# LSH attention with a gated projection on one core: a second weight pair converted in the late stage, and a whole batch taken first there

## The chip, the core and the metric

One core of one Trainium2 chip. It has TensorE (PE) for matrix products, VectorE (DVE), ScalarE (ACT), GpSimd (POOL), and SyncE (SP), whose queue issues most transfers. The metric is the device time of one execution in microseconds.

## The reference

Four batches of 8 heads, 768 tokens and 64 dimensions. q and k are hashed by the signs of six projections; a key counts for a query only where the hashes agree. The softmax over these keys weighs v, and the result, as 3072 rows of 512, goes through a gated projection whose weights come as 64-bit floats.

```
mask = q_bucket[:, :, :, None] == k_bucket[:, :, None, :]
scores = np.where(mask, scale * np.matmul(q, k.transpose(0, 1, 3, 2)), -1000000000.0)
attn = softmax(scores)                       # with 1e-09 in the divisor
x = (attn @ v).transpose(0, 2, 1, 3).reshape(B * S, H * D)
gate = 1.0 / (1.0 + np.exp(-(x @ w_gate)))   # 512 x 1536
return (gate * (x @ w_val)) @ w_out          # 1536 x 512
```

## The kernel before, in words

**Attention (to about 405 us).** 16 pairs of heads, each in two groups of three query tiles. A group has six score tasks on PE (`sc`, eight matmuls, L1551 and L1557), a minimum on DVE for each (L1569), an exponential on ACT (L1578), six tasks of transposes (`tp`, L1614), six copies out of PSUM on ACT or DVE (L1620) and six products with v (`pv`, L1630, four records each in the trace). The result is scaled (L1637) and stored as `xd`.

**Weights.** A tile of 64-bit weights (`raw`) is made into 32-bit floats by `floats` (L674): exponent and mantissa masks (L689, L697) and two combining steps (L702, L707) on DVE, one step on ACT (L692), one product (L712). The float is split into a high and a low part: a cast (L766, L830) and a subtraction (L769, L833). The weights of gate and value come in pairs of blocks (`load_pair`, a pair has two tiles each for gate and value); four sums (L821 to L824) make seven operands of a scheme with seven block products for eight, and the operands are stored in DRAM (`kept_z`, L836). The output weights have one tile for each of 12 blocks (`load_w`); those for later use are stored as `kept`. In attention, masks and combining steps run on DVE and the rest mostly on POOL; in the late stage DVE and ACT do all of it.

There are six pairs of blocks. Of the first pair the plain weights are held as well (`we`), for batch 0. Before, the first five pairs are converted in attention, the last one (`late`, L1221) in the late stage.

**The tail of attention.** Batch 0's products with the first two blocks (`moe_early`: `zg`, `zv`, `zo`) run on PE after the last `pv`. POOL and DVE split x (L867, L870) and the gated blocks (L920) for it.

**The late stage.** For each batch (`products`, L994), the pairs of blocks are visited, first the gate (g), then the value (v). A visit (`visit`, L1166) is seven products of six matmuls (L1178), whose banks ACT copies (L1186) and DVE sums (L1193); then sigmoid (L1250), gating (L1264, L1266) and a split into `gh` and `gl` (L1271, L1274). Between the products of the next two visits stand six output pieces of six matmuls (`y`, L932). The pairs' operands are fetched from DRAM into three slots by POOL's queue (`wsg`, `wsv`, L1728). Batches 1 to 3 are whole (six pairs), batch 0 has five. Before, the order is batch 0, 1, 2, 3, and a whole batch visits the first pair last.

**What sets the order.** Each piece of work is a task with a key, the tasks it follows and the buffers it takes. `Plan.order` (L400) plays the tasks through with fixed times and gives each engine its instructions in one list; PE follows a written list of task numbers, `ORDER` (L51), and `SHIFT` (L113) moves the other keys. On the chip each engine works through its list in order.

Of the kernel before, what the change touches and what calls it, by code (L numbers as in the profile page):

```python
# [507 lines left out]
def lsh_attention_glu_kernel(ctx, tc, q, k, v, proj, w_gate, w_val, w_out, out):  # L508
# [12 lines left out]
    J1 = 2
    NL = 3
    J2 = 10
    JP1, JP2, JPN = J1 // 2, J2 // 2, NJ // 2
    SL = 7
    A11, A21, A12, A22, S1, S2, S4 = range(SL)
    S3 = A21
    SCALE = 1.0 / float(D) ** 0.5
# [1248 lines left out]
```

## Time and profile before

| | us |
|---|---|
| median of 3 runs (964.59 to 965.78) | 965.33 |
| the profiled execution's own time | 965.6 |
| its span, from first to last instruction | 963.8 |
| PE / PE weight loads / DVE / ACT / POOL busy | 952.0 / 774.8 / 608.2 / 548.2 / 274.3 |
| last matmul of attention ends, early products begin | 405.3 |
| first product of the late stage | 428.7 |

The span is the time between the first and the last instruction; 1.8 us of the execution lie around it. Busy shares are means over stages with different limits, so the windows are read by stage. Matmuls are pipelined, and a busy PE can still lose time between kinds of work. The clock of PE was at its full level throughout.

### The profile page before, as it was taken

What the parts mean: (1) busy time and instruction counts of PE and PEld (TensorE: products, weight loads), DVE (VectorE), ACT (ScalarE), POOL (GpSimd) and SP (SyncE); (2) the same over time, 40 slices, a digit from 0 to 9 for tenths busy, and PEclk for the clock granted to TensorE, in tenths of its full rate; (3) what the DMA queues carried; (4) which work ended last, traced back from release to release, by engine and by line L of the source; (5) the groups of instructions that cost most, each with busy time, mean ns of one, the idle gap of its engine ahead of it and who ended that gap; (6) DMA issues with size and microseconds to landing.
All of it is one profiled execution on the core that took longest, in us unless ns stands there. A gap on an engine that the chain in (4) does not pass through costs nothing.

```text
span 963.8 us, 20105 instructions
## 1 busy us (share of the span) xinstructions
PE 952.0 (99%) x8067; PEld 774.8 (80%) x8070; DVE 608.2 (63%) x1173; ACT 548.2 (57%) x993; POOL 274.3 (28%) x325
## 2 busy tenths in 40 slices
PE   9999999999999999999999999999999999999998
PEld 5666665666666567689999999999999999999997
DVE  7999898999899898676656743334633336333332
ACT  5988898898888889554334433324433235333322
POOL 4444655666765665630000000000000000000000
PEclk9999999999999999999999999999999999999999
DMA  7666888888897877489966774444744444644421
GB/s 186 175 194 189 224 252 241 244 249 238 263 268 213 233 228 228 171 315 411 370 237 230 280 262 175 153 153 154 271 170 158 170 177 173 222 154 153 154 78 66
DMA packets 116606, 204.37 MB, mean 212 GB/s; under 512 B 63456, under 2 KB 87968, under 8 KB 110624
## 3 DMA queue, kind: packets, MB, share of 16 engines
q1 hardware_dynamic: 107456, 118.08, 39.9%
q0 software_dynamic: 6688, 84.42, 23.7%
q8 instruction: 63, 1.03, 0.4%
q10 hardware_dynamic: 2368, 0.59, 0.3%
q14 instruction: 31, 0.25, 0.1%
HBM read 147.84 MB, written 43.42 MB: 198 GB/s over the span
## 4 chain that ended last, share of the span: by engine, by line
PE 92%; DVE 4%; DMA 2%; ACT 1%; issue 1%; SPq 0%; ACTq 0%; DVEq 0%
PE y L932 20%; PE pv L1630 12%; PE zBg L1178 10%; PE zBv L1178 10%; PE sc L1557 9%; PE tp L1614 7%; PE zDv L1178 5%; PE zDg L1178 5%; PE sc L1551 4%; PE zAg L1178 2%; PE zAv L1178 2%; PE h L1452 1%; DVE e L1569 1%; PE zg L896 1%; PE zv L896 1%; PE idle L642 1%
## 5 line engine op out<-in xcount | busy, mean ns | idle before, releaser
L1569 DVE TENSOR_SCALAR_CACHE_REDUCE e<-sc 128x768 f32<-128x768 f32 x192 | 177.1, 952 | 20.3 <-PE sc L1557 18.5
L1578 ACT ACTIVATE e<-e,st 128x768 f32<-128x768 f32 x192 | 178.9, 933 | 15.1 <-DVE e L1569 13.2
L932 PE MATMUL y<-wo,gh 128*128 128x512 f32 x480 | 151.0, 396 | 0.0
L1630 PE MATMUL pv<-e,vr 128*64 128x384 f32 x768 | 140.7, 496 | 0.0
L1620 ACT COPY e<-tp 128x768 f32<-128x768 f32 x144 | 112.2, 795 | 27.9 <-PE tp L1614 27.1
L1614 PEld LDWEIGHTS tp<-ident,e 64*128 64x128 f32 x2304 | 87.0, 138 | 45.7 <-issue 13.7
L1178 PE MATMUL zBg<-x,wsg 128*128 128x384 f32 x552 | 111.0, 335 | 0.0
L1178 PE MATMUL zBv<-x,wsv 128*128 128x384 f32 x552 | 110.7, 335 | 0.0
L1178 PEld LDWEIGHTS zBg<-x,wsg 128*128 128x128 f32 x552 | 98.2, 188 | 6.6 <-ACT t1g L1186 0.4
L1178 PEld LDWEIGHTS zBv<-x,wsv 128*128 128x128 f32 x552 | 98.3, 188 | 6.0
L932 PEld LDWEIGHTS y<-wo,gh 128*128 128x128 f32 x480 | 89.9, 187 | 15.2
L1614 PE MATMUL tp<-ident,e 64*128 64x64 f32 x2304 | 99.6, 226 | 1.8 <-DVE e L1569 0.9
L1271 ACT CAST gh<-zt 128x384 fp32r<-128x384 f32 x92 | 47.1, 514 | 95.1 <-DVE zt L1266 75.5
L932 PE MATMUL y<-wo,gl 128*128 128x512 f32 x240 | 93.2, 388 | 0.0
L1557 PE MATMUL sc<-kh,ql 64*128 64x384 f32 x192 | 89.8, 468 | 0.0
L1557 PE MATMUL sc<-kh,qsl 64*128 64x384 f32 x192 | 89.8, 468 | 0.0
L1630 PEld LDWEIGHTS pv<-e,vr 128*64 128x64 f32 x768 | 48.2, 136 | 51.3 <-issue 43.0
L1728 POOL DMA_DIRECT2D wsv<-kzv x23 | 12.2, 532 | 236.9 <-PE zDg L1178 224.6
L1728 POOL DMA_DIRECT2D wsg<-kzg x23 | 12.3, 536 | 227.4 <-PE zDv L1178 206.9
L1250 ACT ACTIVATE sig<-sig 128x384 f32<-128x384 f32 x69 | 36.2, 525 | 61.7 <-DVE sig L1193 61.6
L1274 DVE TENSOR_TENSOR gl<-zt,gh 128x384 fp32r<-128x384 f32 x92 | 51.0, 554 | 29.2 <-ACT gh L1271 29.2
L1551 PE MATMUL sc<-kq 64*128 64x384 bf16 x384 | 64.8, 328 | 2.3 <-ACT e L1620 1.1
(214 smaller groups left out, 1964.4 us busy)
## 6 DMA issues: line engine op xcount, KB each, us to landing
wsg<-kzg POOLq DMA_DIRECT2D x23, 1792.0 KB, 8.1
wsv<-kzv POOLq DMA_DIRECT2D x23, 1792.0 KB, 7.6
kzg<-wkg SPq DMA_DIRECT2D x12, 896.0 KB
kzv<-wkv SPq DMA_DIRECT2D x12, 896.0 KB
rawg<-in_moe_w_gate_dram SPq DMA_DIRECT2D x14, 512.0 KB
rawv<-in_moe_w_val_dram SPq DMA_DIRECT2D x14, 512.0 KB
vr<-in_v_dram SPq DMA_DIRECT2D x16, 384.0 KB
rb<-rd SPq DMA_DIRECT2D x64, 96.0 KB
```

The source lines that it names most:

```text
L932: nc.tensor.matmul(acc, a[:, slot, ts_], w, start=(first and i == 0), stop=(last and i == 2), skip_group_check=cols != slice(None),)
L1178: nc.tensor.matmul(acc, streams[n, jp][:, c, wa, a_], X[x_][:, xa, c], start=first and c == 0 and i == 0, stop=c == 1 and i == 2, skip_gro ...
L1250: lambda blk=blk: nc.scalar.activation(sig[:, blk], w["B"][:, :GN] if blk == 2 else sig[:, blk], AF.Sigmoid),
L1271: nc.scalar.copy(side["h"][:, blk], w["z", blk])
L1274: eng.tensor_sub(side["l"][:, blk], w["z", blk], f(side["h"][:, blk]))
L1551: nc.tensor.matmul(sc[:, j, :GN], kq[z["h"]][rows, 2 + 2 * g + h, t * P : (t + 1) * P], kq[z["h"]][rows, h], start=True, stop=False, tile_ ...
L1557: nc.tensor.matmul(sc[:, j, :GN], q_[rows, c], z["k" + x][rows, h * GN : (h + 1) * GN], start=False, stop=(m == 2), tile_position=(j * D, 0),)
L1569: nc.vector.tensor_scalar(sp(e), gz["sc", t, h][:, :, :GN], -MASKED * SCALE, None, op0=ALU.min, op1=ALU.min, accum_out=gz["st", t][:, h : ...
L1578: nc.scalar.activation(e, e, AF.Exp, bias=st[:, h : h + 1], scale=-1.0, accum_out=gz["su"][:, h * GT + t : h * GT + t + 1],)
L1614: nc.tensor.transpose(tp[:, r, at_ : at_ + D], gz["e", t, h][rows, c * P : (c + 1) * P], ident[rows, rows], tile_position=(r * D, 0),)
L1620: copy(gz["e"][:, :, c * P : (c + 1) * P].rearrange("p n (r d) -> p r n d", r=2), gz["tp", c][:, :, :GN].rearrange("p r (n d) -> p r n d", ...
L1630: nc.tensor.matmul(gz["pv"][rows, :GN], z["v"][:, h, c], gz["e"][:, h * GT : (h + 1) * GT, c * P : (c + 1) * P], start=(c == 0), stop=(c = ...
```

## The change

Four things, and with them new lists `ORDER` and `SHIFT`:

1. `J2` goes from 10 to 8: four of the six pairs are converted in attention, two in the late stage (12 tiles there instead of 6). Their tasks get the key -2 instead of 1000, just ahead of the -1 of the late stage's other DVE work.
2. The late stage takes batch 1, a whole one, first, then 0, 2, 3, and a whole batch visits the pairs in order. The output weights of the first two blocks stay where they are; those of the last two are converted late, stored, and fetched once into the slots of `raw`.
3. The sums of the first pair start from the early weights, high plus low part (`joined`, on POOL), in place of loading and converting the tiles again.
4. The low part is written over the float itself and stored from there, and the float has two buffers; every store is cut into one for the high and one for the low part.

```
-SLOTS = ("two", "one", "e", "st", "su", "sv", "rb", "xs", "vr", "h", "raw2")
+SLOTS = ("two", "one", "e", "st", "su", "sv", "rb", "xs", "vr", "h", "raw2", "mid1", "mid2")
...
-    3, 4, 5, 6, 7, 8, 9, 10, 11, 12, 13, 14, 15, 39, 16, 17, 18, 42, 19, 20, 48, 21, 45, 51, 22, 23, 24, 25, 26, 53,
...
+    3, 4, 5, 6, 7, 8, 9, 10, 11, 12, 13, 14, 15, 16, 39, 17, 18, 19, 42, 20, 21, 22, 48, 45, 51, 23, 24, 25, 26, 27,
...
-    J2 = 10
+    J2 = 8
...
-        raw1=1, mid1=1, raw2=2, mid2=1, wk=1, xr=1, x2=1, x3=1, ob=3,
+        raw1=1, mid1=2, ex1=1, raw2=2, mid2=2, ex2=1, wk=1, xr=1, x2=1, x3=1, ob=3,
...
-            z["all"] = stage().tile([P, SL * P], I32, name=f"mf{name}", tag="wmf", bufs=stock["mid" + own])
+            z["all"] = stage().tile([P, SL * P], I32, name=f"mf{name}", tag=f"wmf{slot['mid' + own]}", bufs=1)
...
-        early = j if j < J1 else j - NJ + J1 if j >= NJ - J1 else None
+        early = j if j < J1 else None
...
+        away = last and n == "o" and j >= NJ - J1
...
+                z["h"] = (later["w"] if last else stage1).tile([P, SL * P], F32R, name=f"w{n}{j}", tag="wk", bufs=1)[:, :N_EL]
+            if "w" in z:
+                z["h"], z["l"] = z["w"][:, 0], z["w"][:, 1]
+            else:
+                z["l"] = z["mf"].bitcast(F32R)
...
+        elif away:
+            s_ = [
+                dma(key, 262144, lambda: keep(0), after=[h]),
+                dma(key, 262144, lambda: keep(1), after=[made[n, j]], give=["mid" + own]),
+            ]
+            add(FIRST, "sp", 0, lambda: None, after=[s_[0], made[n, j]], give=["wk2"])
+            made[n, j] = dma(1e3, 524288, fetch, after=[*s_, *everything], take=["raw2"])
+        else:
...
+            y["l"] = y["f"].bitcast(F32R)
+            eng.tensor_sub(y["l"], y["f"], f(y["h"]))
...
+        def joined():
+            z["all"] = stage1.tile([P, SL * P], I32, name=f"mf{n}{jp}_{c}", tag=f"wmf{slot['mid1']}", bufs=1)
+            of = streams["e"][:, "gv".index(n)].rearrange("p j a (h c m) -> a c p h j m", h=2, m=P)
+            to = f(z["all"])[:, :N_EL].rearrange("p (h j m) -> p h j m", h=2, j=2)
+            for h in range(2):
+                nc.gpsimd.tensor_add(to[:, h], f(of[0, c])[:, h], f(of[1, c])[:, h])
+
+        if jp < JP1:
+            z, own = {}, "1"
+            e = add(key, "pool", 1340, joined, after=[made[n, 0], made[n, 1]], take=["mid1"], port=0.92)
+        else:
+            z, e, own = floats(key, load, [last or score_tasks[at_n]], last, f"{n}{jp}_{c}")
...
+        s_ = [dma(key, 458752, lambda: keep(0), after=[h]), dma(key, 458752, lambda: keep(1), after=[m], give=["mid" + own])]
+        add(FIRST, "sp", 0, lambda: None, after=[s_[0], m], give=["wk2" if last else "wk"])
...
-        jps = list(range(JP1, JPN)) + list(range(JP1)) * whole_
+        jps = list(range(JP1 * (not whole_), JPN))
...
+                    for w_ in line:
+                        if len(w_) == 2:
+                            load_w(-2, *w_, False, m1)
+                        else:
+                            everything.append(load_pair(-2, *w_, m1))
...
-    for b in range(B):
-        prev = products(2e4 + b, b, prev, ends)
+    for m, b in enumerate([B - NL, *range(B - NL), *range(B - NL + 1, B)]):
+        prev = products(2e4 + m, b, prev, ends)
```

The lists move instructions on every engine. At the end of attention, on PE, before (`tp` are transposes, `pv` products with v; the numbers are batch, group and chunk):

```order
L1614 MATMUL tp_3_0_2_7382<-ident,e_3_0_7048 128x64 x12
L1614 MATMUL tp_3_0_3_7396<-ident,e_3_0_7048 128x64 x12
L1630 MATMUL pv_3_0_7373<-e_3_0_7048,vr_3_7001 64x384 x2
L1614 MATMUL tp_3_1_0_7420<-ident,e_3_1_7245 128x64 x12
L1614 MATMUL tp_3_0_4_7436<-ident,e_3_0_7048 128x64 x12
L1630 MATMUL pv_3_0_7373<-e_3_0_7048,vr_3_7001 64x384 x2
L1614 MATMUL tp_3_1_1_7455<-ident,e_3_1_7245 128x64 x12
L1614 MATMUL tp_3_1_2_7468<-ident,e_3_1_7245 128x64 x12
L1614 MATMUL tp_3_1_3_7482<-ident,e_3_1_7245 128x64 x12
L1630 MATMUL pv_3_0_7373<-e_3_0_7048,vr_3_7001 64x384 x2
L1630 MATMUL pv_3_1_7502<-e_3_1_7245,vr_3_7001 64x384 x6
L1614 MATMUL tp_3_0_5_7517<-ident,e_3_0_7048 128x64 x12
```

and after, at the same place:

```order
L1665 MATMUL tp_3_0_1_7271<-ident,e_3_0_7029 128x64 x12
L1665 MATMUL tp_3_0_2_7285<-ident,e_3_0_7029 128x64 x12
L1681 MATMUL pv_2_1_7061<-e_2_1_6809,vr_2_6579 64x384 x2
L1681 MATMUL pv_3_0_7303<-e_3_0_7029,vr_3_6990 64x384 x4
L1681 MATMUL pv_2_1_7061<-e_2_1_6809,vr_2_6579 64x384 x2
L1681 MATMUL pv_3_0_7303<-e_3_0_7029,vr_3_6990 64x384 x2
L1665 MATMUL tp_3_0_3_7315<-ident,e_3_0_7029 128x64 x12
L1665 MATMUL tp_3_1_0_7331<-ident,e_3_1_7178 128x64 x12
L1665 MATMUL tp_3_0_4_7346<-ident,e_3_0_7029 128x64 x12
L1681 MATMUL pv_2_1_7061<-e_2_1_6809,vr_2_6579 64x384 x2
L1681 MATMUL pv_3_0_7303<-e_3_0_7029,vr_3_6990 64x384 x2
L1665 MATMUL tp_3_1_1_7367<-ident,e_3_1_7178 128x64 x12
```

The products with v stand in fewer and longer runs; over the whole of attention PE changes its kind of work 383 times before and 368 times after, up to the first product of the late stage.

On DVE in the late stage, the gate visit whose sums have the most conversion work around them, before (`sig` are the sums that free a bank of PE, the others convert weights):

```order
L1193 TENSOR_TENSOR sig<-zAg_0_8390,t1g_0_8403 128x384
L689 TENSOR_SCALAR exv_0_8420<-rawv_0_8160 128x512
L697 TENSOR_SCALAR mfv_0_8423<-rawv_0_8160 128x512
L702 SCALAR_TENSOR_TENSOR mfv_0_8423<-rawv_0_8160,mfv_0_8423 128x512
L707 SCALAR_TENSOR_TENSOR exv_0_8420<-rawv_0_8160,exv_0_8420 128x512
L712 TENSOR_TENSOR mfv_0_8423<-mfv_0_8423,exv_0_8420 128x512
L821 TENSOR_TENSOR mfv_0_8423<-mfv_0_8423 128x128
L822 TENSOR_TENSOR mfv_0_8423<-mfv_0_8423 128x128
L823 TENSOR_TENSOR mfv_0_8423<-mfv_0_8423 128x128
L824 TENSOR_TENSOR mfv_0_8423<-mfv_0_8423 128x128
L1193 TENSOR_TENSOR sig<-zDg_0_8426,t167g_0_8452 128x384
L1193 TENSOR_TENSOR sig<-zDg_0_8426,t16g_0_8434 128x384
```

and after, in the fifth pair of the first batch:

```order
L1241 TENSOR_TENSOR sig<-zAg_1_8537,t1g_1_8544 128x384
L732 SCALAR_TENSOR_TENSOR exg_0_8494<-rawg_0_8405,exg_0_8494 128x512
L737 TENSOR_TENSOR mfg_0_8548<-mfg_0_8548,exg_0_8494 128x512
L863 TENSOR_TENSOR mfg_0_8548<-mfg_0_8548 128x128
L864 TENSOR_TENSOR mfg_0_8548<-mfg_0_8548 128x128
L865 TENSOR_TENSOR mfg_0_8548<-mfg_0_8548 128x128
L866 TENSOR_TENSOR mfg_0_8548<-mfg_0_8548 128x128
L714 TENSOR_SCALAR exo_8590<-rawo_8484 128x512
L722 TENSOR_SCALAR mfo_8592<-rawo_8484 128x512
L876 TENSOR_TENSOR mfg_0_8548<-mfg_0_8548,wkg_8588 128x896
L727 SCALAR_TENSOR_TENSOR mfo_8592<-rawo_8484,mfo_8592 128x512
L1241 TENSOR_TENSOR sig<-zDg_1_8569,t167g_1_8603 128x384
```

Between a visit's first and second sum (`zAg`, `zDg`) stand ten instructions in place of nine, now with a low part and steps of the next tile in one row, and in the whole of the second to fifth pair 93 conversion instructions beside the 56 own ones, and two for x.

On POOL at the end of attention, before (`mf`, `wk`: conversion of the first pair; `gl`, `xh`, `xl`: the early products; `wsg`: the first fetch of the late stage):

```order
L821 TENSOR_TENSOR mfg_0_7506<-mfg_0_7506 128x128
L822 TENSOR_TENSOR mfg_0_7506<-mfg_0_7506 128x128
L823 TENSOR_TENSOR mfg_0_7506<-mfg_0_7506 128x128
L824 TENSOR_TENSOR mfg_0_7506<-mfg_0_7506 128x128
L830 CAST wkg_7574<-mfg_0_7506 128x896
L833 TENSOR_TENSOR wkg_7574<-mfg_0_7506,wkg_7574 128x896
L920 TENSOR_TENSOR gl<-gf_0_0_7643,gh 128x384
L867 CAST xh_1_7659<-xr_1_2591 128x384
L870 TENSOR_TENSOR xl_1_7660<-xr_1_2591,xh_1_7659 128x384
L867 CAST xh_1_7659<-xr_1_2591 128x384 x3
L870 TENSOR_TENSOR xl_1_7660<-xr_1_2591,xh_1_7659 128x384
L1728 DMA wsg_46_7712<-kzg_130 128x3584
```

and after:

```order
L1636 TENSOR_SCALAR su_148<-su_148 128x6
L1636 TENSOR_SCALAR su_149<-su_149 128x6
L976 TENSOR_TENSOR gl<-gf_0_0_7540,gh 128x384
L923 CAST xh_1_7553<-xr_1_2520 128x384
L926 TENSOR_TENSOR xl_1_7554<-xr_1_2520,xh_1_7553 128x384
L923 CAST xh_1_7553<-xr_1_2520 128x384
L926 TENSOR_TENSOR xl_1_7554<-xr_1_2520,xh_1_7553 128x384
L1779 DMA wsg_46_7580<-kzg_130 128x3584
```

No conversion is left there, and the fetch stands two casts and a split earlier.

## Rows read from the trace of the kernel before

**Rows 1.** The page, part 1: busy us, share of the span, instructions.
```profile
PE 952.0 (99%) x8067; PEld 774.8 (80%) x8070; DVE 608.2 (63%) x1173; ACT 548.2 (57%) x993; POOL 274.3 (28%) x325
```

**Rows 2.** Windows: PE, PEld, DVE, ACT, POOL busy us (instructions); clock; DMA share; GB/s.
```profile
14.00:405.00 391.00, 385.62 (x5080) 253.76 (x5078) 351.58 (x704) 339.03 (x598) 233.67 (x250) 1.00 0.77 225
430.00:540.00 110.00, 109.96 (x579) 102.43 (x578) 69.23 (x131) 50.87 (x93) 6.36 (x11) 1.00 0.78 300
540.00:950.00 410.00, 410.00 (x2149) 381.77 (x2148) 160.28 (x285) 139.62 (x273) 17.49 (x33) 1.00 0.49 176
```

**Rows 3.** Waits of the weight loads from 428 us on: total, times, longest.
```profile
PEld zBg L1178 <- ACT t1g L1186: 0.4, 1, 0.4
```

**Rows 4.** Timeline of PE near 390 us: start, us, what, form, count.
```profile
383.51 0.36 PE L1551 MATMUL sc<-kq 64*128 64x384 bf16 x2
384.21 0.36 PE L1551 MATMUL sc<-kq 64*128 64x384 bf16 x2
386.14 3.45 PE L1630 MATMUL pv<-e,vr 128*64 128x384 f32 x20
389.52 0.59 PE L1614 MATMUL tp<-ident,e 64*128 64x64 f32 x12
395.87 0.87 PE L1630 MATMUL pv<-e,vr 128*64 128x384 f32 x4
396.66 1.35 PE L1614 MATMUL tp<-ident,e 64*128 64x64 f32 x36
397.94 2.80 PE L1630 MATMUL pv<-e,vr 128*64 128x384 f32 x16
```

**Rows 5.** Groups by form, DVE, 0 to 405 us: busy, mean ns, idle before.
```profile
L689 DVE TENSOR_SCALAR exg<-rawg 128x512 int32<-128x512 int32 x12 | 6.9, 575 | 0.0
L697 DVE TENSOR_SCALAR mfg<-rawg 128x512 int32<-128x512 int32 x12 | 6.7, 556 | 0.0
L702 DVE SCALAR_TENSOR_TENSOR mfg<-rawg,mfg 128x512 f32<-128x512 uint32 x12 | 8.2, 684 | 0.2
L707 DVE SCALAR_TENSOR_TENSOR exg<-rawg,exg 128x512 int32<-128x512 int32 x12 | 8.2, 687 | 0.2 <-ACT exg L692 0.2
```

**Rows 6.** Timeline of PE, an early output product that waits.
```profile
416.13 0.50 PE L932 MATMUL zo<-wo,gl 128*128 128x512 f32 x1 [0.98 <-DVE gl L920]
```

**Rows 7.** Groups by form, DVE, 430 to 540 us.
```profile
L689 DVE TENSOR_SCALAR exg<-rawg 128x512 int32<-128x512 int32 x2 | 0.8, 420 | 0.0
L712 DVE TENSOR_TENSOR mfg<-mfg,exg 128x512 f32<-128x512 f32 x2 | 1.4, 692 | 0.1
L821 DVE TENSOR_TENSOR mfg<-mfg 128x128 f32<-128x128 f32 x2 | 0.6, 293 | 0.1
L833 DVE TENSOR_TENSOR wkg<-mfg,wkg 128x896 fp32r<-128x896 f32 x2 | 2.2, 1093 | 0.4 <-ACT wkg L830 0.3
L1193 DVE TENSOR_TENSOR sig<-zDg,t167g 128x384 f32<-128x384 f32 x5 | 2.8, 556 | 6.2 <-ACT t167g L1186 6.2
```

**Rows 8.** Timeline of POOL, three stream fetches.
```profile
457.90 0.53 POOL L1728 DMA_DIRECT2D wsv<-kzv  x1 [9.54 <-PE zDg L1178]
480.82 0.53 POOL L1728 DMA_DIRECT2D wsv<-kzv  x1 [10.93 <-PE zDg L1178]
513.35 0.53 POOL L1728 DMA_DIRECT2D wsv<-kzv  x1 [12.31 <-DMA kzv<-wkv]
```

**Rows 9.** Groups by form, ACT, 430 to 540 us.
```profile
L830 ACT CAST wkg<-mfg 128x896 fp32r<-128x896 f32 x2 | 1.9, 940 | 0.0
```

**Rows 10.** The chain that ended last, two pieces: start, us, what.
```profile
457.60 1.39 PE y L932 x6
461.07 1.39 PE y L932 x6
```

**Rows 11.** Timeline of SP, the last late store of a pair.
```profile
509.20 0.32 SPq L836 DMA_DIRECT2D kzv<-wkv  x1
```

**Rows 12.** DMA issues, 405 to 560 us: count, KB, median us to landing.
```profile
wsv<-kzv POOLq DMA_DIRECT2D x7, 1792.0 KB, 9.5
```

More of the change, by code (lines that the diff above doesn't have):

```diff
@@ L714, in floats @@
         a = dma(key, 524288, load_, slack=3000 if last else 2500, after=after, take=[place])
-        b1 = add(key, "dve", 336, exponent, after=[a], take=["mid" + own], port=0.92)
+        b1 = add(key, "dve", 336, exponent, after=[a], take=["ex" + own], port=0.92)
         b2 = add(key, "act", 628, shifted, after=[b1])
-        c1 = add(key, "dve", 400, mantissa, after=[b1], port=0.92)
+        c1 = add(key, "dve", 400, mantissa, after=[b1], take=["mid" + own], port=0.92)
         c2 = add(key, "dve", 605, whole, after=[c1], port=0.92)
@@ L720, in floats @@
         return z, add(
-            key, "dve" if last else "pool", 680 if last else 1240, lambda: scaled(nc.vector if last else nc.gpsimd), after=[d], port=0.92
+            key, "dve" if last else "pool", 680 if last else 1240, lambda: scaled(nc.vector if last else nc.gpsimd), after=[d], give=["ex" + own], port=0.92
         ), own
@@ L753, in load_w @@
         z, e, own = floats(key, load, [last or score_tasks[at_n]], last, f"{n}{j}")
+        away = last and n == "o" and j >= NJ - J1
         def high():
-            if early or last:
+            if early or last and not away:
                 if n == "o":
@@ L768, in low, with keep @@
+            (nc.scalar.copy if last else nc.gpsimd.tensor_copy)(z["h"], f(z["mf"]))
         def low(eng):
-            eng.tensor_sub(z["w"][:, 1], f(z["mf"]), f(z["w"][:, 0]))
-        def keep():
-            nc.sync.dma_start(kept[n, j], f(z["w"]))
+            eng.tensor_sub(z["l"], f(z["mf"]), f(z["h"]))
+        def keep(m):
+            nc.sync.dma_start(kept[n, j][:, m], f(z["hl"[m]]))
         def fetch():
-            w = home(j)
+            w = later["w"].tile([P, 2, N_EL], F32R, name=f"wo{j}", tag=f"wraw{slot['raw2']}", bufs=1) if away else home(j)
@@ L776, in fetch @@
             weights[n, j] = w[:, 0], w[:, 1]
             nc.sync.dma_start(f(w), kept[n, j])
-        h = add(key, "act" if last else "pool", 525 if last else 590, high, port=0 if last else 0.92, after=[e] + (g_free if last else []), take=[] if early or last else ["wk"])
+        h = add(key, "act" if last else "pool", 525 if last else 590, high, port=0 if last else 0.92, after=[e], take=["wk2"] if away else [] if early or last else ["wk"])
         made[n, j] = add(
             key, "dve" if last else "pool", 629 if last else 1236, lambda: low(nc.vector if last else nc.gpsimd), port=0.92,
-            after=[h], give=["mid" + own],
+            after=[h], give=["mid" + own] if early or last and not away else [],
@@ L783, in load_w @@
         )
         if not early and not last:
-            a = dma(key, 524288, keep, after=[made[n, j]], give=["wk"])
-            fetches[n, j] = (a, fetch)
-        elif early and n == "o":
-            kept_early.append(dma(key + 20, 524288, keep, after=[made[n, j]]))
+            s_ = [
+                dma(key, 262144, lambda: keep(0), after=[h]),
+                dma(key, 262144, lambda: keep(1), after=[made[n, j]], give=["mid" + own]),
+            ]
+            add(FIRST, "sp", 0, lambda: None, after=[s_[0], made[n, j]], give=["wk"])
@@ L790, in stream @@
+            fetches[n, j] = (s_, fetch)
+        elif away:
+            s_ = [
+                dma(key, 262144, lambda: keep(0), after=[h]),
+                dma(key, 262144, lambda: keep(1), after=[made[n, j]], give=["mid" + own]),
+            ]
+            add(FIRST, "sp", 0, lambda: None, after=[s_[0], made[n, j]], give=["wk2"])
+            made[n, j] = dma(1e3, 524288, fetch, after=[*s_, *everything], take=["raw2"])
+        else:
+            everything.append(made[n, j])
     def stream(n, jp):
@@ L842, in load_pair @@
         m = add(key, [("dve", 1005, lambda: low(nc.vector))] if last else
[L843 removed]
+                [("pool", 2078, lambda: low(nc.gpsimd)), ("dve", 1005, lambda: low(nc.vector))], after=[h], port=0.92)
         made.setdefault((n, jp, "p"), []).append(m)
[L845 removed]
+        s_ = [dma(key, 458752, lambda: keep(0), after=[h]), dma(key, 458752, lambda: keep(1), after=[m], give=["mid" + own])]
+        add(FIRST, "sp", 0, lambda: None, after=[s_[0], m], give=["wk2" if last else "wk"])
+        keeps.setdefault((n, jp), []).extend(s_)
         return h
@@ L1001, in products @@
         whole_ = b >= B - NL
-        jps = list(range(JP1, JPN)) + list(range(JP1)) * whole_
+        jps = list(range(JP1 * (not whole_), JPN))
         visits = [(jp, n) for jp in jps for n in "gv"]
-        if b == B - NL:
-            for j in range(J1):
-                def again(j=j):
-                    w = later["w"].tile([P, 2, N_EL], F32R, name=f"wo{j}l", tag=f"wraw{slot['raw2']}", bufs=1)
-                    weights["o", j] = w[:, 0], w[:, 1]
-                    nc.sync.dma_start(f(w), kept["o", j])
-                made["o", j] = dma(1e4, 524288, again, after=kept_early + [prev, made["o", NJ - 1]] + g_free, take=["raw2"])
         X = {}
@@ L1720, in switch @@
         later["ps"] = ctx.enter_context(tc.tile_pool(name="ps3", bufs=2, space=PSUM))
-    later["switch"] = add(0, "sp", 0, switch, after=every + [a for a, _ in fetches.values()] + [a for k_ in keeps.values() for a in k_],
+    later["switch"] = add(0, "sp", 0, switch, after=every + [a for k_, _ in fetches.values() for a in k_] + [a for k_ in keeps.values() for a in k_],
                           give=["moe"] * 3 + [r for r, n in late_stock.items() for _ in range(n)])
```

41 lines of the change are left out of this document (17 added, 24 removed), and 601 rows, old and new, of tables (ORDER, SHIFT).

## The prediction

> **What bounds the kernel now.** I read the page's busy shares first, then windows by stage, then the waits, then the timeline of single stretches. TensorE (PE) is busy for 952.0 of 963.8 us [rows 1]. The windows split that into two regimes [rows 2]. From 540 to 950 us PE is busy for 410.00 of 410 us and VectorE (DVE) for 160.28, so DVE has room there. From 430 to 540 us, where the weights of the last block pair are converted beside the products, DVE has 69.23 of 110 us and PE still 109.96. The waits agree: from 428 us on the longest wait of a weight load is 0.4 us, once [rows 3]. In the late stage, then, the time is the matmuls' own, and the change leaves their number and shapes as they are: 23 block pairs with 2 visits of 42 product matmuls, and 36 output matmuls for each pair. The late stage can only lose.
>
> What can be won lies between 14 and 405 us, in attention. The window shows PE busy for 385.62 of 391 us [rows 2], but pipelined matmuls hide small waits, so I make a ledger from pitches [rows 4]. A score task (8 matmuls) takes 384.21 - 383.51 = 0.70 us. A `pv` product shows as four records; 20 records take 389.52 - 386.14 = 3.38 and 4 take 396.66 - 395.87 = 0.79, so four records cost (3.38 - 0.79)/4 = 0.65 and leaving `pv` for transposes 0.14 more. Three transpose chunks with the change into `pv` take 397.94 - 396.66 = 1.28; with 0.1 for the change, a choice, a chunk is 0.39. There are 192 of each (16 head pairs x 2 groups x 6): 134 + 125 + 75 = 334 us. The turning of q and k (30 times a chunk) and 15 hashes (8 matmuls at the pitch of `pv`, 0.16, and half as much again for their change) add 12 + 10, and PE's changes of kind (75 runs of `pv`, some 83 entries into `pv` or hash) 11 + 8. That is 375 to 377, I take 377; 391 - 377 leaves about 14 us in which PE waits in pieces, most of them under 0.3 us. This estimate is the pool from which the change can draw.
>
> **The change part by part.** The profiled run took 965.6 us, of which 963.8 are span; the median of the runs shown is 965.33, so 0.3 comes off at the end.
>
> *PE's order in attention.* Before, PE changes its kind of work 383 times up to the first late product, after it 368 times; the runs of `pv` fall from 75 to 72. Three changes out of `pv` are 0.4 us, all fifteen at 0.14 would be 2.1. I take 1.0 off, since most of the fifteen are between scores and transposes, which cost little.
>
> *DVE in attention.* Conversions there fall from 34 to 24 tiles: four go because the first pair's sums are formed from the early weights, six because a pair more is converted late. Each takes the four DVE instructions of [rows 5]: 575 + 556 + 684 + 687 = 2.50 us, so 25 us. Other rows change engine (four more transposed chunks, one more set of sums and three more low parts on DVE, seven copies of q and k fewer); counted in the order these add about 2. DVE goes from 351.6 to about 329 of 391 us [rows 2], its idle share from 10% to 16%. The last conversion now follows score 150 of 192, before it followed the last score, so the relief lies mostly at the end. How PE's 14 us answer no row shows. The ends are nothing gained (the waits are for ScalarE or DMAs) and all 14. I let them shrink as DVE's idle share grows, 14 x 10/16 = 9, and take 5 off.
>
> Here the Trainium skill speaks otherwise: Perfetto Trace Analysis, section Identifying the Most-Contended Engine, says that matmul busy time is a bad measure for TensorE, that weight-load busy is a better one, and that the engine with the highest occupancy is the one to relieve. In this window weight loads have 253.76 of 391 us, 65%, and DVE 90% [rows 2], so by that rule attention is DVE's and 23 us off DVE would bring the whole kernel to about 946. The ledger does not agree: PE's own pitches fill 377 of the 391.
>
> *The tail of attention.* GpSimd (POOL) no longer converts there. Before, PE waited 0.98 us for the low part of a gated early block [rows 6]; afterwards the same chain of multiply, cast and subtraction stands in front of the same first output product, so I take 0. Cover for x, the first stream and the operands are the same 132 early matmuls, in a slightly other order. Bounds: -1.5 and +1.5.
>
> *DVE in the late stage.* Now two pairs are converted there, 12 tiles. With [rows 7] a tile of gate or value costs two masks at 0.42, three steps at 0.69 (the product's row stands for all three), four sums at 0.29 and the low part at 1.09: 5.2 us. One of output weights has no sums and a shorter low part, 3.6. A block pair takes PE 480.82 - 457.90 = 22.92 us between fetches that wait for it [rows 8]; in it DVE has 14 own instructions of 0.556 [rows 7], 7.8 us. Reading the new order from one first sum to the next, the second to fifth pairs hold 11.4 (two x operands among them), 11.7, 14.1 and 14.0 us beside these, in all 19.2, 19.5, 21.9 and 21.8 of 22.92. Before, the fullest of these pairs held 18.9, with no wait. So DVE runs at 95% for two pairs, and behind each blocked instruction the next sum waits, and for the sum the bank that PE writes next. The low part stands behind its four sums in DVE's queue and waits for ScalarE's cast, 0.94 us [rows 9], while nothing else can pass.
>
> I walked these pairs by hand. PE does two products and an output piece in 461.07 - 457.60 = 3.47 us, 1.39 of it the piece [rows 10], so a sum may end up to 2.4 us after its product. The first sum of the fourth pair comes 0.5 us late, that of the fifth 0.8; in the fifth, one low part and two output steps stand before the second sum, which is 1.5 late, and the value half loses 0.6. That is 3.4 us. Ends: 0 (DVE hides it as it did at 82%), and 10 by the first rival. ScalarE has 50.87 of 110 us [rows 2] and covers its own six casts more.
>
> *Stores and streams.* Each store is cut into a high and a low half, and the low part now stands in the buffer that the next but one conversion overwrites, so DVE's mantissa step waits for a store to land. A whole store took 513.35 - 509.20 = 4.15 us until POOL could fetch it [rows 8, 11]; the nearest such pair of instructions lies 5 to 6 us apart in the fifth pair. Covered, by 1 to 2 us. The last stored half precedes its visit by some 16 us, against those 4.15 and a fetch of 9.5 [rows 12]: covered by 2. The whole batch first costs nothing by itself.
>
> Sum: -1.0 - 5 + 0 + 3.4 = -2.6; 965.6 - 2.6 = 963.0, against the median 962.7.
>
> **The rivals.** *Late DVE does not keep up (slower).* If the cast stands open before all 12 low parts, at about 1 us, the four pairs ask 82.4 + 12 = 94.4 of PE's 4 x 22.92 = 91.7: 3 more than the 3.4, and the last store then comes too late for its stream, some 4 more. Late cost 10, gain in attention 4: about 971. It decides once the late stage loses more than attention's 6. For it: DVE at 95% in a fixed order; against: stretches at 82% without any wait.
>
> *DVE was the bound of attention (fast).* Nearly all 14 us go, order 1, late cost 2: 965.3 - 13 + 2 = 954. For it: DVE at 90%, and the rule above; against: the ledger, and the first 150 scores stay almost as densely filled with conversions (24 in 150 against 34 in 192).
>
> *Nothing is gained.* Attention's waits are made by the order itself, so only 1 to 2 us go, and the late stage takes them back: 965. That the change doesn't unburden DVE can be excluded by the order.
>
> **How the numbers follow.** No change means within 0.2%, 963.4 to 967.3, about what can be told here. Forecast 0.44, by itself 959.5 to 966.5: three in five of it faster, a third same, the rest slower. Slow rival 0.22, slower. Fast rival 0.16, faster. Nothing gained 0.18: mostly same, a tenth faster, the rest slower. Faster 0.26 + 0.16 + 0.02 = 0.44; same 0.15 + 0.14 = 0.29; slower 0.27. The range 956 to 970 leaves out the outer parts of the fast and the slow rival.
>
> **What would show it.** PE's first early-weight matmul (405.3 us before) near 399.5, with DVE about 329 us busy from 14 to there. From 430 to 545 us DVE near 100 us busy instead of 69, and PE waits of together 3 to 4 us on ScalarE's copies and DVE's sums in the fourth and fifth pair; none before or after. If the first matmul comes at 404 or later, or late waits exceed 6 us, I am wrong in that term; if PE waits for a `wsg` or `wsv` fetch, the covers of the streams were wrong.

## The result, and the profile after

The changed kernel takes 975.93 us (median of 4 runs, 973.65 to 977.37) against 964.96 us for the kernel before (4 runs, 963.84 to 965.78): ratio 1.0112, 95% interval 1.0088 to 1.0136. It is slower, and above the range. The profiled execution after has a span of 975.6 us against 963.8, 11.8 more. I first looked at where these arise. The windows of after, with the columns of [rows 2] (PE, PEld, DVE, ACT, POOL busy, clock, DMA share, GB/s):

```profile
14.00:405.00 391.00, 381.17 (x5059) 251.35 (x5058) 336.01 (x668) 328.77 (x586) 201.84 (x217) 1.00 0.69 199
430.00:540.00 110.00, 105.95 (x547) 97.72 (x546) 76.87 (x153) 50.55 (x93) 7.07 (x11) 0.98 0.88 322
540.00:950.00 410.00, 409.35 (x2142) 380.23 (x2140) 173.86 (x308) 147.37 (x285) 18.46 (x35) 1.00 0.53 190
```

DVE did lose work in attention (351.58 to 336.01 us), but PE is busy for 4.5 us less there, and for 4 us less between 430 and 540, at a mean clock of 0.98. The timeline of PE gives the seams. After:

```profile
408.38 0.44 PE L952 MATMUL zg<-xh,we 128*128 128x384 f32 x1
431.76 1.16 PE L1226 MATMUL zBg<-x,wsg 128*128 128x384 f32 x5
971.37 0.40 PE L988 MATMUL y<-wo,gh 128*128 128x256 f32 x2
```

Before, the last two seams were:

```profile
428.75 0.51 PE L1178 MATMUL zBg<-x,wsg 128*128 128x384 f32 x2
959.61 0.40 PE L932 MATMUL y<-wo1l,gh 128*128 128x256 f32 x2
```

Attention ends 3.1 us later (408.38 against 405.32). From there to the first late product both take 23.4 us, but after, six of the early matmuls (three `zv` at 0.17 and three `zo` at 0.23 us) stand behind that product, so the tail lost 1.2. The late stage, to the start of the last matmul (0.1 us behind the start of the rows shown), takes 539.7 instead of 531.0 us, 8.7 more, of which these six matmuls are 1.2. So 3.1 + 1.2 + 7.5 = 11.8.

Where in the late stage, windows by block pair show; second to sixth pair of the first batch, same columns:

```profile
455.60:478.50 22.90, 22.90 (x121) 21.33 (x120) 17.80 (x34) 9.48 (x19) 1.05 (x2) 1.00 0.94 354
478.50:501.40 22.90, 22.90 (x121) 21.32 (x121) 16.55 (x36) 9.47 (x18) 0.75 (x1) 1.00 0.80 292
501.40:524.30 22.90, 22.90 (x122) 21.32 (x121) 19.16 (x42) 11.49 (x20) 1.06 (x2) 1.00 0.77 260
524.30:552.80 28.50, 25.03 (x122) 22.51 (x121) 19.95 (x42) 10.90 (x20) 0.76 (x2) 0.94 0.75 274
552.80:576.90 24.10, 23.45 (x121) 21.01 (x120) 16.37 (x27) 12.69 (x23) 1.87 (x4) 1.00 0.88 328
```

The fifth pair takes 28.5 us for the 22.9 of the others: 5.6 of the 7.5 us. The sixth loses 1.2, and the remaining 0.7 lie mostly at the stage's start. The waits of PE from 428 us on (columns as in [rows 3]):

```profile
PE zDg L1226 <- DVE sig L1241: 3.1, 1, 3.1
PE zBg L1226 <- ACT t16g L1234: 0.8, 2, 0.4
PE zBg L1226 <- ACT t167g L1234: 0.4, 1, 0.4
PE zBv L1226 <- ACT t16v L1234: 0.3, 1, 0.3
```

One wait of 3.1 us for a sum on DVE. In the timeline of DVE the sum stands behind this:

```profile
527.34 0.42 DVE L714 TENSOR_SCALAR exo<-rawo 128x512 int32<-128x512 int32 x1
531.30 0.43 DVE L722 TENSOR_SCALAR mfo<-rawo 128x512 int32<-128x512 int32 x1 [3.53 <-DMA kzg<-mfg]
531.64 1.08 DVE L876 TENSOR_TENSOR mfg<-mfg,wkg 128x896 fp32r<-128x896 f32 x1
```

The mantissa mask of an output-weight tile writes the buffer from which the low half of an earlier tile is being stored (`kzg<-mfg`). DVE had room, but nothing in its queue can pass the mask. The store's issue on SP, and what POOL issued between the two halves:

```profile
521.28 0.32 SPq L879 DMA_DIRECT2D kzg<-wkg  x1
523.08 0.32 SPq L879 DMA_DIRECT2D kzg<-mfg  x1
```

```profile
521.87 0.53 POOL L1779 DMA_DIRECT2D wsv<-kzv  x1 [12.53 <-DMA kzv<-mfv]
```

This low half of the store (448 KB) lands 8.2 us after its issue, 10.0 us after that of the high half; between the two halves a stream fetch of 1792 KB begins. Before, 896 KB landed in 4.15 us, and no stream ran, since the next fetch waited for that very store [rows 8, 11]. A second loss follows: from 534 to 540 us the mean granted clock is 0.72, which is 3.4 us at the lower level (6 x 0.28 / 0.5); PE had stood for 3.1 us just before. Two products of six matmuls show it, the first inside, the second behind:

```profile
534.00:540.00 6.00, 6.00 (x24) 5.47 (x25) 1.65 (x3) 2.01 (x5) 0.53 (x1) 0.72 0.86 283
```

```profile
537.33 1.83 PE L1226 MATMUL zBv<-x,wsv 128*128 128x384 f32 x6
538.99 1.20 PE L1226 MATMUL zAv<-x,wsv 128*128 128x384 f32 x6
```

In attention, the waits of the transposes' weight loads for DVE's score minima have doubled. Before and after:

```profile
PEld tp L1614 <- DVE e L1569: 10.8, 24, 1.2
```

```profile
PEld tp L1665 <- DVE e L1620: 21.2, 35, 3.3
```

The longest is at 239 us; the timeline of DVE and POOL ahead of it, then PE's row:

```profile
233.63 0.43 DVE L714 TENSOR_SCALAR exo<-rawo 128x512 int32<-128x512 int32 x1 [1.15 <-DMA rawo<-in_moe_w_out_dram]
235.28 1.02 DVE L722 TENSOR_SCALAR mfo<-rawo 128x512 int32<-128x512 int32 x1 [1.22 <-DMA kzv<-mfv]
236.10 1.87 POOL L1440 TENSOR_TENSOR ql<-rawq,qh 128x768 fp32r<-128x768 f32 x1
236.22 0.55 DVE L1688 TENSOR_TENSOR xs<-pv,rb 128x384 f32<-128x384 f32 x1
236.69 1.83 DVE L727 SCALAR_TENSOR_TENSOR mfo<-rawo,mfo 128x512 f32<-128x512 uint32 x1
238.44 0.94 DVE L1620 TENSOR_SCALAR_CACHE_REDUCE e<-sc 128x768 f32<-128x768 f32 x1
```

```profile
239.45 0.34 PE L1665 MATMUL tp<-ident,e 64*128 64x64 f32 x4 [2.62 <-DVE e L1620]
```

Three things meet in one row of DVE's queue: a load that is late, the new wait for a low-half store, and a combining step of 1.83 us instead of 0.69. Behind them stands the minimum that frees PE's bank. This is the worst case: in the four other profiles with the same attention PE waits there twice, 0.7 to 0.8 and 0.95 us.

### The profile page after: what moved, and what is told of

It is laid out like the page before. It is cut to its first block, busy times and chain, and to the rows that moved or that the text cites. A ratio compares the mean times of both kernels' runs of the same rounds, so it can differ in the third digit from the quotient of the medians.

```text
span 975.6 us, 20111 instructions
## 1 busy us (share of the span) xinstructions
PE 954.5 (98%) x8066; PEld 774.6 (79%) x8070; DVE 616.2 (63%) x1188; ACT 547.1 (56%) x995; POOL 242.0 (25%) x292
## 4 chain that ended last, share of the span: by engine, by line
PE 84%; DVE 6%; POOL 3%; DMA 2%; ACT 2%; issue 2%; SPq 1%; DVEq 0%; POOLq 0%; ACTq 0%
PE y L988 19%; PE pv L1681 11%; PE zBv L1226 10%; PE zBg L1226 9%; PE sc L1608 7%; PE tp L1665 6%; PE zDg L1226 5%; PE zDv L1226 5%; PE sc L1602 3%; PE zAv L1226 2%; PE zAg L1226 2%; DVE e L1620 2%; PE idle L667 1%; DMA kzg<-mfg 1%; PE h L1503 1%
## 5 line engine op out<-in xcount | busy, mean ns | idle before, releaser
L1620 DVE TENSOR_SCALAR_CACHE_REDUCE e<-sc 128x768 f32<-128x768 f32 x192 | 176.4, 952 | 18.4 <-PE sc L1608 14.9
L988 PE MATMUL y<-wo,gh 128*128 128x512 f32 (+1 forms) x556 | 174.5, 396 | 0.0
L1665 PEld LDWEIGHTS tp<-ident,e 64*128 64x128 f32 x2304 | 86.0, 138 | 50.9 <-DVE e L1620 21.2
L1671 ACT COPY e<-tp 128x768 f32<-128x768 f32 x140 | 108.9, 793 | 29.2 <-PE tp L1665 28.4
L988 PEld LDWEIGHTS y<-wo,gh 128*128 128x128 f32 x556 | 104.3, 188 | 17.6
L988 PE MATMUL y<-wo,gl 128*128 128x512 f32 (+1 forms) x278 | 107.8, 388 | 0.0
```

What stands on the lines that cost most here:

```text
L988: nc.tensor.matmul(acc, a[:, slot, ts_], w, start=(first and i == 0), stop=(last and i == 2), skip_group_check=cols != slice(None),)
L1620: nc.vector.tensor_scalar(sp(e), gz["sc", t, h][:, :, :GN], -MASKED * SCALE, None, op0=ALU.min, op1=ALU.min, accum_out=gz["st", t][:, h : ...
L1665: nc.tensor.transpose(tp[:, r, at_ : at_ + D], gz["e", t, h][rows, c * P : (c + 1) * P], ident[rows, rows], tile_position=(r * D, 0),)
L1671: copy(gz["e"][:, :, c * P : (c + 1) * P].rearrange("p n (r d) -> p r n d", r=2), gz["tp", c][:, :, :GN].rearrange("p r (n d) -> p r n d", ...
```

## The experiments

All but two kernels keep the order of the instructions that remain. In the table, "attention" is the start of the first early-weight matmul, "late" the time from the first late product to the start of the last matmul, both from the profile; the median is of all runs.

| | attention | late | median | ratio to before, 95% |
|---|---|---|---|---|
| before | 405.3 | 531.0 | 964.96 | |
| after | 408.4 | 539.7 | 975.93 | 1.0088 to 1.0136 |
| late_room | 406.5 | 538.5 | 974.38 | 1.0079 to 1.0132 |
| late_room_light | 405.5 | 538.8 | 975.27 | 1.0083 to 1.0160 |
| no_stream | 406.1 | 535.1 | 971.74 | 1.0059 to 1.0108 |
| late_fix | 407.9 | 536.6 | 970.81 | 1.0047 to 1.0092 |
| att_light | 401.4 | 538.2 | 968.96 | 1.0033 to 1.0068 |
| att_dma | 402.7 | 537.0 | 969.36 | 1.0036 to 1.0070 |
| att_port | 404.0 | 538.5 | 971.98 | 1.0063 to 1.0111 |
| after_att_none | 398.0 | 538.1 | 965.63 | 0.9995 to 1.0023 |
| before_att_light | 404.5 | 531.0 | 964.82 | 0.9995 to 1.0021 |
| before_att_none | 399.6 | 531.0 | 960.77 | 0.9949 to 0.9976 |
| raw2 | 435.0 | 534.9 | 998.31 | 1.0331 to 1.0365 |
| slack5 | 418.6 | 535.6 | 983.78 | 1.0181 to 1.0220 |

### The late stage: a store, or too much work on DVE?

**late_room**: the mask no longer waits for the store.

```
-            z["all"] = stage().tile([P, SL * P], I32, name=f"mf{name}", ...)
+            z["all"] = mp.tile([P, DM], I32, name=f"mf{name}", tag="ob", ...) if last and name[0] == "o" else stage().tile(...)
```

> The changed kernel with its order kept to the last instruction; only the mantissa of a late output-weight tile lies in a buffer of its own (one of the three output buffers, which are idle then), so its mask waits for no store. Theory S (the late stage lost its time to a store wait): VectorE's 3.5 us wait for a low-half store at 531 us goes, with it TensorE's 3.1 us wait and the 3.4 us at half clock behind it; the late stage is some 5.5 us shorter, about 970.4 us against 975.9. Theory D (VectorE has too much work for two pairs): the blocked work only moves, and the time stays within 1.5 us of 975.9. Neither moves the end of attention, 408.4 us.

DVE's wait is gone, the time hardly moves. PE now waits 2.4 us at the same place for ScalarE, whose timeline shows:

```profile
527.59 0.94 ACT L872 CAST wkg<-mfg 128x896 fp32r<-128x896 f32 x1 [3.31 <-DMA kzg<-wkg]
```

The high half's buffer is the next one that the same store holds, and the copy that frees PE's bank stands behind this cast. So the expectation of 970.4 failed, and the store remains the suspect. Behind the 2.4 us the clock falls again (0.62 from 530 to 533 us):

```profile
530.78 2.29 PE L1226 MATMUL zDg<-x,wsg 128*128 128x384 f32 x6
```

**late_room_light**: late_room with two combining steps and the product left out of every late conversion.

> As late_room, and in the late stage the two combining steps and the product of every conversion are left out (3 x 0.69 us for each of 12 tiles, 25 us of VectorE's work), so the weights converted late are wrong. Theory S: little more is gained than in late_room, 1 to 3 us, to 967.5 to 969.5. Theory D: this is where the loss goes, with late_room near 975.9 and this one near 967. A third way, a loss that neither shortens (fetches, or order on TensorE): both stay above 972.

DVE is busy for 84.0 instead of 106.7 us in 151 us from the late stage's start, and nothing is gained (975.27). PE still waits 3.3 us at the same place for ScalarE, so DVE's load does not make this wait. The third way that the expectation names is what came.

**no_stream**: after, without the stream fetch that runs beside the store.

```
+        skip = ends["first"] and (n, jp) == ("v", JP2)
...
-            nc.gpsimd.dma_start(f(to), kept_z[n, jp])
+            streams.update({(n, jp): streams["g", jp]}) if skip else nc.gpsimd.dma_start(f(to), kept_z[n, jp])
```

> The changed kernel with one fetch left out: the value operands of the fifth pair in the first batch (1792 KB, issued at 521.9 us between the two halves of a store); the gate's operands are used again, so this visit's products are wrong. In late_room the wait only moved, to ScalarE's cast, which waited 3.3 us for the same store's high half (issued 519.3, landed 527.6). Theory S2 (a store of 448 KB lands 8 us after its issue because the fetch runs beside it; 896 KB took 4.15 us alone in the kernel before): it lands within 5 us, both waits go, TensorE's 3.1 us wait and the 3.4 us at half clock with them, the late stage is 4.5 to 5.5 us shorter, the time about 971. Rival (the store is slow by itself, or its queue is full): VectorE's wait stays above 2.5 us and the time within 1.5 of 975.9.

The waits on both engines are gone; this is the whole list of PE's waits from 428 us on:

```profile
PE zBg L1226 <- ACT t16g L1234: 0.8, 2, 0.4
PE zBg L1226 <- ACT t167g L1234: 0.4, 1, 0.4
PE zBv L1226 <- ACT t16v L1234: 0.3, 1, 0.3
```

The late stage is 4.6 us shorter, and the clock stays at its upper level through it. It is still 4.1 us longer than in the kernel before: 1.2 are the six early matmuls, 0.6 lie at its start, 0.9 in the fifth pair and 1.4 in the sixth. The list shows 1.5 of these 2.9 as small waits for ScalarE's copies; what makes them no run tests.

**late_fix**: all transfers and all work stay; both buffers that the store holds are doubled where it matters.

```
+            y["h"] = (
+                later["w"].tile([P, 2, 2, SL, P], F32R, ..., tag="ws2")[:, 0, 0] if (n, jp, c) == ("g", JPN - 1, 0)
+                else stage().tile([P, SL * P], F32R, ..., tag="wk", bufs=1).rearrange("p (s m) -> p s m", s=SL))
```

> The changed kernel, output as the reference's, order kept to the last instruction; in the late stage the mantissa of an output-weight tile lies in an idle output buffer, and the high part of one tile (gate, fifth of the late pairs' eight operands, the one whose cast waited in late_room) in the stream slot that its own pair is fetched into later. So nothing in VectorE's and ScalarE's queues waits for the store that the stream fetch slows down. Theory S2: the late stage is 4.5 to 5 us shorter, as without the fetch (no_stream, 971.7), and the time 970.5 to 972. Rival (in no_stream it was the missing traffic as such that helped, other transfers too): 974 or more.

The time, 970.81, is in the expected range, but in part by luck: the late stage (536.6) gains 3.1 us and not the 4.5 to 5 expected. The profiled run, at 973.92, is the slowest of four; if its late stage holds for the other three (970.52 to 970.82), their attention ended near 404.8, an estimate. A new wait for a sum on DVE appears some 16 us further on; it is most of what the late stage lacks against no_stream. It begins at the next store: ScalarE's cast of a value tile finds its buffer still held by a store of output weights, and DVE's low part and that sum stand behind the cast. PE's wait, then ScalarE's row:

```profile
PE zAg L1226 <- DVE zt L1241: 1.2, 1, 1.2
```

```profile
543.55 0.94 ACT L872 CAST wkv<-mfv 128x896 fp32r<-128x896 f32 x1 [3.57 <-DMA ko<-wo]
```

### Attention: what does DVE's work cost?

**before_att_light** and **att_light**: the two combining steps left out in attention.

```
-            nc.vector.scalar_tensor_tensor(f(z["mf"]), z["low"]...
+            last and nc.vector.scalar_tensor_tensor(f(z["mf"]), z["low"]...
-            nc.vector.scalar_tensor_tensor(z["ex"], z["high"], SIGN...
+            last and nc.vector.scalar_tensor_tensor(z["ex"], z["high"], SIGN...
```

> The kernel before with the same two steps of its 34 conversions in attention left out (34 x 1.38 = 47 us of VectorE's work), weights wrong, the rest of the order kept. By the step of the forecast (waits shrink in proportion to VectorE's idle share) the first early-weight matmul comes from 405.3 to about 397, the time to 957. If VectorE is the bound of attention, to 392 and 952 or less. If load on VectorE hardly matters at a kept order, it stays above 403, and the time above 963.

> The changed kernel with the two combining steps of the 24 conversions in attention left out on VectorE (24 x 1.38 = 33 us, more than the 25 us that the change took off it), weights wrong, the rest of the order kept. If TensorE's waits in attention come from VectorE being late, the first early-weight matmul comes from 408.4 to 399 us or earlier and the time falls by 9 or more, to 967 or less. If attention is held by TensorE's own list, by ScalarE or by transfers, it stays within 2 us of 408.4, and the time within 2 us of 975.9.

In the kernel before, DVE falls from 351.58 [rows 2] to 309.10 us, and attention ends 0.8 us earlier; the median does not move (964.82, and 964.54 for the kernel before, run beside it):

```profile
14.00:405.00 391.00, 386.09 (x5083) 254.26 (x5082) 309.10 (x637) 338.81 (x598) 232.75 (x251) 1.00 0.77 225
```

In the kernel after, 35 us less bring 7.0 (4.1 against the earliest end of the unchanged order, 405.5), and the waits for minima fall back from 21.2:

```profile
PEld tp L1665 <- DVE e L1620: 13.5, 29, 1.0
```

So before the change DVE's load did not matter; after it, it does.

**before_att_none** and **after_att_none**: conversions emptied (33 of 34, and all but the first ones of 24).

```
-            load(raw)
+            z["again"] or (load(raw), last or filled.update(raw=raw))
...
-            nc.vector.tensor_scalar(z["ex"], z["high"], 0x7FF00000, ...)
+            last or filled.update(ex=z["ex"]); z["again"] or nc.vector.tensor_scalar(z["ex"], z["high"], 0x7FF00000, ...)
```

> The kernel before, where 33 of the 34 conversions in attention lose their load, their four VectorE steps, the ScalarE step and the product on GpSimd (84 us of VectorE's 352, 24 of ScalarE's), values wrong; casts, sums, low parts and stores stay, order kept. If the 14 us of waits of the ledger come from any of these, the first early-weight matmul comes from 405 to 398 or earlier. If they are in TensorE's own order and the chain of scores, minimum, exponential, transposes and copies, it stays above 402, and the time above 961.

> The changed kernel with the conversions in attention emptied as in before_att_none: after the first tiles no load of 64-bit weights, none of the four VectorE steps, no ScalarE step, no product on GpSimd, values wrong; sums, casts, low parts and stores stay, and the order with them; the late stage is the changed kernel's. It measures the new lists of attention by themselves. By the forecast's term for TensorE's order (1 us) the first early-weight matmul comes at 398.6 us, against 399.6 in before_att_none; then the 2 to 9 us between the two attentions with conversions are made by conversions that stand closer to what TensorE waits for. If the new lists are worse by themselves, it comes at 401 or later. The time then follows with the late stage as it is, 966 and 968.5.

```profile
399.57 0.44 PE L896 MATMUL zg<-xh,we 128*128 128x384 f32 x1
```

```profile
398.04 0.44 PE L952 MATMUL zg<-xh,we 128*128 128x384 f32 x1
```

By themselves the new lists are 1.5 us better. With conversions 5.7 us come on top before (405.3; by the medians of runs made side by side, 964.25 and 960.77, it is 3.5) and 7.5 to 10.4 after (405.5 to 408.4), though there are ten conversions fewer.

**att_dma** and **att_port**: in after, the 64-bit weights loaded once, and the mantissa of output weights in its own buffer; and GpSimd's subtraction replaced by a copy.

```
-            load(raw)
+            filled and not last or (load(raw), last or filled.update(raw=raw))
```

```
-                eng.tensor_sub(z[n + "l"], z["raw", n], f(z[n + "h"]))
+                eng.tensor_copy(z[n + "l"], z["raw", n]) if eng is nc.gpsimd else eng.tensor_sub(...)
```

> The changed kernel with the transfers of the conversions in attention taken out of VectorE's way, order kept: the 64-bit weights are loaded once and used for all 24 tiles (values wrong), and the mantissa of output-weight tiles has a buffer of its own. Theory T1 (VectorE stands for late loads and stores, 5.1 us in the profile after): the first early-weight matmul comes from 405.5 to 408.4 (three profiles with this attention) to 403 or less, the time to 972 or less. Theory T2 (the order on VectorE: four conversion steps in a row ahead of a score's minimum, whose bank TensorE needs): it stays within 405 to 408.5, and the time at 974 to 976.

> The changed kernel with GpSimd's subtraction that makes the low part of q and k (1.83 us) replaced by a copy of one input, values wrong, order kept. At 62 to 65, 236 to 240 and 260 to 264 us VectorE's combining steps took 1.3 to 1.95 us instead of 0.69 beside that subtraction, and TensorE waited 1.4 to 3 us behind them. If the two engines get into each other's way there, these steps come back to 0.7 to 1.0 us and the first early-weight matmul to 403 or less, time 972. If the number of steps in a row alone makes the waits, it stays within 405 to 408.5.

att_dma brings attention to 402.7, as theory T1 said; it takes the waits and 12 MB of traffic away at once, and does not tell these apart. att_port brings it to 404.0, short of the 403 expected. PE's waits for minima ahead of transposes, in after, att_dma and att_port:

```profile
PE tp L1665 <- DVE e L1620: 5.7, 6, 2.6
PE tp L1665 <- DVE e L1620: 2.8, 4, 1.3
PE tp L1665 <- DVE e L1620: 1.9, 5, 0.7
```

att_dma removes the wait at 239 us and keeps those near 66 and 265 us (1.28 and 1.08); att_port brings all of them to 0.7 or less. In att_port the step that took 1.83 us at 236 us takes 0.85:

```profile
234.16 0.85 DVE L727 SCALAR_TENSOR_TENSOR mfo<-rawo,mfo 128x512 f32<-128x512 uint32 x1
```

That alone would prove nothing, for late_fix keeps the subtraction and has 0.84 there; there the next step pays:

```profile
236.48 0.84 DVE L727 SCALAR_TENSOR_TENSOR mfo<-rawo,mfo 128x512 f32<-128x512 uint32 x1
238.12 1.43 DVE L732 SCALAR_TENSOR_TENSOR exo<-rawo,exo 128x512 int32<-128x512 int32 x1
```

Clearer are two steps that are long in all profiles with the subtraction. After, then the same two in att_port:

```profile
63.98 1.44 DVE L732 SCALAR_TENSOR_TENSOR exv<-rawv,exv 128x512 int32<-128x512 int32 x1
261.52 2.17 POOL L1440 TENSOR_TENSOR ql<-rawq,qh 128x768 fp32r<-128x768 f32 x1
262.38 1.95 DVE L732 SCALAR_TENSOR_TENSOR exg<-rawg,exg 128x512 int32<-128x512 int32 x1
```

```profile
63.45 0.68 DVE L732 SCALAR_TENSOR_TENSOR exv<-rawv,exv 128x512 int32<-128x512 int32 x1
257.85 1.28 POOL L1440 CAST ql<-rawq 128x768 fp32r<-128x768 f32 x1
258.83 0.84 DVE L732 SCALAR_TENSOR_TENSOR exg<-rawg,exg 128x512 int32<-128x512 int32 x1
```

So the transfers stand behind the wait at 239 us, and GpSimd's subtraction behind most of those near 66 and 265 us.

**raw2** and **slack5**: on late_fix, the load a tile earlier with a second buffer, or counted as landing later; here the planner gives DVE, ACT, POOL and SP new lists beside PE's old one.

```
-        raw1=1, mid1=2, ...
+        raw1=2, mid1=2, ...
```

```
-        a = dma(key, 524288, load_, slack=3000 if last else 2500, ...)
+        a = dma(key, 524288, load_, slack=3000 if last else 5000, ...)
```

> late_fix, and in attention a second buffer for the 64-bit weights (in a tile that is idle there), known to the planner, so that a load is issued a tile earlier, and the output-weight mantissa in its own buffer; TensorE's order is kept, the planner moves some 120 instructions on each other engine. Theory T1 (VectorE stands for late loads and for stores; att_dma brought the first early-weight matmul to 402.7 us): 404 or earlier, time 968.5 or less. Theory T2 (only less work on VectorE or a lucky order helps): 405 to 408.5, time 970.5 to 973.

> late_fix, and the planner counts each load of 64-bit weights in attention as landing 2.5 us later than before, so that the first mask stands further back in VectorE's queue; one buffer as in the changed kernel, TensorE's order kept. Theory T1: VectorE's waits for loads (3.7 us in the profile after) go and the first early-weight matmul comes at 404 or earlier, time 968.5 or less. Theory T2: it stays within 405 to 408.5, time 970.5 to 973; worse than that if conversions now arrive late elsewhere.

Both fail by far: attention ends 27 and 11 us later than in late_fix, while their late stages are as short as without the fetch. They are no test of T1, since all the other engines' lists moved with the load. That these no longer fit PE's list is my reading; what is shown is that new lists beside the old one cost 11 and 27 us, as much as the conversions themselves or more. No version tried that does all the work beats the kernel before.

## Why the prediction was wrong, step by step

**PE's order in attention**, -1.0: borne out in size. With the conversions emptied the difference is -1.5, which also holds the casts, sums and stores of ten tiles fewer.

**DVE in attention**, -5: this step failed, and it is the larger error. I wrote "I let them shrink as DVE's idle share grows, 14 x 10/16 = 9, and take 5 off". The relief was there, though only 15.6 us in the window of [rows 2] (336.01, not about 329), but the waits do not follow DVE's idle share. In the kernel before, 42.5 us off DVE are worth at most 0.8 us, and emptying the conversions on every engine is worth 3.5 to 5.7 of my 14; the rest stays without them. I had noted that the relief lies mostly at the end, and that the first 150 scores stay as densely filled; I gave it a value all the same. What decides, as I read the rows, is where a conversion stands in DVE's queue, and the new lists put blocked or slowed ones right ahead of minima that PE waits for; no run that moved a conversion alone shows it. The sum had -1.0 and -5, and attention gave +0.2 to +3.1 (its end varies from 405.5 to 408.4 over five profiles with this attention). If each profiled end is shifted by its run's distance from the median, an estimate, attention ends at 404.0 to 405.0 before and 404.8 to 407.4 after: a loss of some 2 us in place of a gain of 6. The rule that I set against my step, from the Trainium skill, Perfetto Trace Analysis, section Identifying the Most-Contended Engine, would have erred more: relieving the engine with 90% brought 0.8 us. "Nothing is gained" came nearest for this stage, which did not even keep its time.

**The tail**, 0 with bounds of 1.5: it lost 1.2, inside the bounds.

**DVE in the late stage**, +3.4: the place (fifth pair) was right, the mechanism not. I counted 19.2, 19.5, 21.9 and 21.8 us of DVE's time per pair; the windows show 17.80, 16.55, 19.16 and 19.95. The count was right, the adding was not: consecutive instructions overlap (the one at 236.22 us above takes 0.55, the next one starts after 0.47). The durations in these windows add up to 19.5, 18.4, 21.4 and 22.2, which overstates DVE's busy time by 10 to 12%. DVE was at 72 to 84% of 22.9 us before the fifth pair, not at 95. From 430 to 545 us it was busy for 81.5 us, not the 100 that I expected. late_room_light excludes its load as the cause of the long wait. Without that wait (no_stream) 2.9 us remain, near my 3.4 in size, but in small waits of which the list names ScalarE's copies and no sum on DVE.

**Stores and streams**: this step failed. "Covered, by 1 to 2 us" rested on 4.15 us for a whole store, measured where no stream ran. With a stream beside it and its other half also under way, half of that volume took 8.2, and the cover, 4.7 us from the issue to the mask's turn where I had read 5 to 6, was short by 3.5. That is the wait of 3.1 us on PE, and with the lower clock and the small waits around it 5.6. The row on which I rested it said so itself: that store was what the fetch waited for [rows 8], so the two could not overlap there; in the new order they do. My other cover, of the last stored half for its fetch, held: PE waited for no fetch.

**The rivals.** "Late DVE does not keep up", at 971, came nearest in sign and size, and its late cost of 10 is close to 8.7; its cause, a cast open before every low part, is not what happened. The sign of my forecast was wrong on two counts: the gain of 6 that I counted on did not exist, and even with it the 8.7 us of the late stage would have made the kernel slower by 2.7.

What stays open is which part of the transfers costs attention more, the waits on late loads and stores or the traffic itself, and what the 2.9 us of the late stage are.

## What to carry to other kernels

In an engine's queue ask first what each instruction that reuses a buffer waits for, and who stands behind it; a store that releases a buffer must be priced with the transfers that will run beside it in the new order, not with a row where it ran alone. Freed time on a busy engine is worth nothing until a wait of the bounding engine is traced to it; a run that empties the suspected work at a kept order tells that in one try. And giving one store's buffer a double moved the wait to the next buffer of the same store, and doubling that one moved part of it to the next store: find all that they hold.

## What the runs showed of the hardware

- A store of 448 KB on SP's queue, its other half issued 1.8 us before, landed after 8.2 us beside a fetch of 1792 KB on POOL's queue; without that fetch the waits for it vanished (no_stream). The Trainium skill, DMA: Bandwidth & Descriptors, section Issuing engines are not separate DMA queues, says that transfers from all issuing engines interleave on the same 16 DMA engines; these rows agree.
- After a wait of 3.1 us PE's granted clock was at the lower level (1.2 GHz) for 3.4 us, and a product of six matmuls took 1.83 us instead of 1.2. In late_room a wait of 2.4 us in the same products had 3.4 us at the lower level behind it as well. It did not fall after 1.2 us in late_fix, nor in attention after 2.62 us at 239 us, where the mean of the next 4 us is 1.00:

```profile
240.00:244.00 4.00, 3.79 (x70) 2.75 (x66) 3.96 (x7) 4.00 (x9) 3.41 (x4) 1.00 0.72 228
```

- DVE's combining step took 0.69 us alone. Begun while GpSimd's subtraction was under way it took 1.83 us (at 236 us) and 1.95 us (at 262 us), and ended 0.55 and 0.64 us after the subtraction; begun during the shorter copy of att_port it took 0.84 and ended 0.54 us after the copy. The Trainium skill, SBUF — State Buffer, section SBUF: two separate sides, says that the two engines hold a shared pair of ports for a whole instruction; these numbers agree with it.
- The same order of instructions ended attention anywhere between 405.5 and 408.4 us over five profiles.
